# A linear-attention and feed-forward kernel on one core: its beginning in another order, and three operations on other engines

## The chip, the core and the metric

One core of a Trainium2 chip runs the whole program. The metric is the time of one execution on the device in microseconds (us), as a median over several executions; a profile of one execution shows what each engine did. The engines here are TensorE (PE, with its weight loads as PEld), VectorE (DVE), ScalarE (ACT), GpSimd (POOL) and SyncE (SP), which issues transfers; ACT's queue can issue transfers too (ACTq).

## The reference

```python
# attention: B=4, H=8, S=768, D=48
f = sigmoid(f_logit)
for t in range(S):
    state = f[:, :, t, :, None] * state + einsum('bhd,bhde', k[:, :, t], v[:, :, t])
    y[:, :, t] = einsum('bhd,bhde->bhe', q[:, :, t], state)
# feed-forward on x = y as (3072 tokens, 384 channels); d_ff = 1536
out = ((x @ w_a) * (x @ w_b)) @ w_out
```

q, k, v and f_logit come as 32-bit floats; w_a, w_b and w_out come as 64-bit floats (two 32-bit words each) and the kernel turns them into 32-bit floats itself.

## The kernel before

All work that runs is in `by_quotients` (a second function, `by_levels`, is a fallback for other data). The attention is cut into 16 **units** (4 batches, 2 halves of 384 tokens, 2 groups of 4 heads), numbered 0 to 15; two units make one **block** of 384 tokens for the feed-forward, so there are 8 blocks. Unit u's inputs lie in one of four sets of tiles (`f_in`, `k_in`, `q_in`, `v_in`).

A unit goes through these steps. `front(u)` has three parts: two sigmoids on ACT (L211, L212) and two products on POOL (L214, L215); then `fix` on ACT (L217), a running product of f on DVE (L220, a scan, two halves of 384 columns), a check value `held` (L221) and the product that scales q (L222), both on DVE; then a second scan (L226) and the product that scales k (L227) on DVE. `scores(u)` is 48 small matmuls (L251) into the PSUM tile `ps_x` and a product with a causal mask on DVE (L259). `turn(u)` transposes k on PE (L275) and copies it on ACT (L277 or L279). `gains(u)` makes the states (PE L294, DVE L308 to L317). `within(u)` (L327) and `across(u)` (L347) add up y in `ps_y`; ACT copies it out (L358) into the one buffer `y`, and five transfers (L372) put it into `xT`, which the feed-forward reads.

The weights come as 36 **pieces** of 128 by 384 values: 12 times one of w_b and one of w_a, then 12 of w_out. A piece is loaded into a `raw` tile by SP (`load_weights`, L153). `from_double` converts it in three stages, a generator that is advanced once per step of `conversion`: first |hi| and the sign on ACT (L165, L166) and a clamp on POOL (L167); then three operations on DVE (L171, L172, L173), an addition on POOL (L174) and |h| on ACT (L175); then the product with the sign on DVE (L178). A step of `conversion` starts one new piece, takes the second stage of the one before and the third of the one before that, and issues one further load, four pieces ahead. `convert(n)` runs steps until n pieces are done.

`ffn(blk)` has 12 steps for the two products (L387: w_b, then w_a), each ended by a copy `b_sb` on ACT (L395) and a product `ab` on DVE (L397), and then the product with w_out (L407), copied out (L417) and stored (L419, SP). In block 0 the conversion runs beside the feed-forward, two pieces per step at first and then one, and the w_out product goes by pieces too. The attention steps of the later units are put between the steps by a list of numbers (`queue`).

Every engine works through its own list in the order in which the code emits it, and so does SP with its transfers: one that has to wait holds all behind it. The code around the change is the beginning, which is written out by hand (L453 to L503):

```python
for _ in range(4): load_weights()
...
convert(0); next(fronts[0]); next(fronts[0]); scores(0); turn(0, True)
convert(1); next(fronts[1]); next(fronts[1]); within(0); gains(0)
for u in range(NQ, NSET): load_unit(u)
next(fronts[2]); scores(1); turn(1, True)
```

Of the kernel before, what the change touches and what calls it, by code (L numbers as in the profile page):

```python
# [10 lines left out]
FP32 = mybir.dt.float32  # L11
# [62 lines left out]
def by_quotients(ctx, tc, q, k, f_logit, v, moe_w_a, moe_w_b, moe_w_out, out, ident, weights, bad):  # L74
# [131 lines left out]
    def front(u):  # L206
# [35 lines left out]

    def scores(u):
        t = sets[u % NSET]
        qf, kf = halves(t["q"]), halves(t["k"])
        ps = ps_x
        for n, c, o in each():
            for h in range(2):
                for p in range(2):
                    r = slice(R * h, R * h + D)  # L250
                    nc.tensor.matmul(  # L251
                        ps[SUB * p:SUB * p + SUB, h, o:o + SUB],
                        lhsT=kf[r, tokens(n, c, p)],
                        rhs=qf[r, tokens(n, c, p)],
                        start=True,
                        stop=True,
                    )
        at = sb2.tile([128, 2, BLK], FP32, tag="at", name="at")
        nc.vector.tensor_tensor(  # L259
            at.rearrange("s h (o t) -> s h o t", t=SUB),  # L260
            ps[:, :, 0:BLK].rearrange("s h (o t) -> s h o t", t=SUB),
            causal.unsqueeze(1).unsqueeze(1).broadcast_to((128, 2, 2 * NC, SUB)),
            ALU.mult,
        )
        live[u]["at"] = at

    def turn(u, spare=False):

        kf = halves(sets[u % NSET]["k"])
        kT = sb1.tile([128, 2, NC, 128], FP32, tag="kT", name="kT")  # L270
        for n in range(2):
            ps = ps_f.tile([128, 512], FP32, tag="f", name="f") if spare else ps_x[:, n]
            for c in range(NC):
                o = n * BLK + c * C
                nc.tensor.transpose(ps[:, c * C:c * C + C], kf[:, o:o + C], ident)  # L275
            if spare:
                nc.scalar.copy(kT[:, n].rearrange("s c x -> s (c x)"), ps[:, 0:BLK])  # L277
# [58 lines left out]
    def across(u):  # L336
# [116 lines left out]
    with tc.manual_schedule():  # L453
        nc.scalar.preload_act_table_set("sigmoid_and_others")
        for x, value in ((less, -K_EXP), (two, 2.0), (zeros, 0.0)):
            nc.gpsimd.memset(x, value)
        for i in range(NSET):
            for n, eng, x in (("f", nc.vector, 30.0), ("k", nc.gpsimd, 0.0), ("q", nc.vector, 0.0)):
                eng.memset(sets[i][n], x)
            if i < NQ:  # L460
                load_unit(i, "f")
            if i == 0:
                make_identity(nc, ident)
        for u in range(NQ):
            load_unit(u, "kqv")
# [19 lines left out]
        next(fronts[0])
# [400 lines left out]
```

## Time and profile before

| | us |
|---|---|
| median of three runs (lowest, highest) | 754.71 (754.36, 755.13) |
| the profiled execution, its own time | 754.88 |
| its span, first to last instruction | 752.80 |
| PE busy | 643.6 (85%) |
| DVE busy | 277.3 (37%) |
| ACT busy | 182.6 (24%) |
| POOL busy | 114.0 (15%) |

The profiled execution took 2.08 us more than its span. A busy share is an average over stages that differ: in forty slices of the span PE is at 0 to 6 tenths in the first seven and at 9 tenths from the thirteenth on. The first matmul of the feed-forward (L387) starts at 83.44 us, and that of its second block at 213.26 us.

### The profile page before, as it was taken

Reading aid. Unit: us, or ns where it says so; the run is one execution under the profiler, and the core shown is the slowest. Engines: PE = TensorE matmul, PEld = TensorE weight load, DVE = VectorE, ACT = ScalarE, POOL = GpSimd, SP = SyncE. Lnnn points to the kernel's source line nnn. Section 1 sums busy time; section 2 is a strip of 40 time slices with the busy share of each in tenths; the row PEclk is TensorE's granted clock in tenths of the full one; section 3 lists DMA queues with packets and bytes.
Section 4 is the critical chain, followed back from the end, with each engine's and each line's share of the span. In section 5 each row is a group of like instructions: output and inputs, shape, how many; then the busy total and the mean of one; then the engine's idle time right before and its main releaser. Section 6 shows DMA issues by size and latency. Waiting matters only on the chain.

```text
span 752.8 us, 11345 instructions
## 1 busy us (share of the span) xinstructions
PE 643.6 (85%) x4770; PEld 392.3 (52%) x4770; DVE 277.3 (37%) x484; ACT 182.6 (24%) x343; POOL 114.0 (15%) x121
## 2 busy tenths in 40 slices
PE   0322665576989999999999999999999999999996
PEld 0312333343556666666666666665665666555553
DVE  7716867775933331334024313322342211101100
ACT  2232344443422211222022202221221111011100
POOL 5221454445520100110011001100101000000000
PEclk9655699879999999999999999999999999999999
DMA  8166333532421022012301040103000100010000
GB/s 209 44 157 166 83 89 104 149 100 84 125 79 43 7 77 66 10 39 60 84 0 49 27 115 1 49 6 105 1 18 1 37 11 17 1 38 11 1 11 24
DMA packets 34300, 43.29 MB, mean 58 GB/s; under 512 B 4032, under 2 KB 32704, under 8 KB 34240
## 3 DMA queue, kind: packets, MB, share of 16 engines
q1 hardware_dynamic: 29888, 37.76, 18.6%
q10 hardware_dynamic: 4352, 4.72, 2.4%
q8 instruction: 39, 0.64, 0.3%
q14 instruction: 21, 0.17, 0.1%
HBM read 33.03 MB, written 4.72 MB: 50 GB/s over the span
## 4 chain that ended last, share of the span: by engine, by line
PE 72%; POOL 9%; DVE 7%; ACT 4%; issue 4%; DMA 1%; ACTq 1%; SPq 1%; DVEq 0%; POOLq 0%
PE f L387 44%; PE f L407 22%; POOL h L174 6%; PE ps_x L251 2%; POOL h L167 2%; PE ps_y L327 2%; ACT h L165 1%; PE ps_y L347 1%; DVE r L173 1%; PE ps_x L294 1%; PE ps_x L275 1%; DVE f_in L220 1%; DVE r L172 1%; POOL fix L215 1%; ACTq L372 1%
## 5 line engine op out<-in xcount | busy, mean ns | idle before, releaser
L387 PE MATMUL f<-xT,w_b 128*128 128x384 f32 x576 | 214.4, 510 | 23.2 <-ACT b_sb L395 23.2
L387 PE MATMUL f<-xT,w_a 128*128 128x384 f32 x576 | 202.0, 487 | 0.0
L407 PE MATMUL f<-w_out,ab 128*128 128x384 f32 x576 | 190.3, 488 | 5.3 <-DVE w_out L178 3.5
L397 DVE TENSOR_TENSOR ab<-f,b_sb 128x384 f32<-128x384 f32 x96 | 53.5, 558 | 334.2 <-PE f L387 296.2
L387 PEld LDWEIGHTS f<-xT,w_b 128*128 128x128 f32 x576 | 110.7, 198 | 97.9 <-ACT b_sb L395 26.9
L407 PEld LDWEIGHTS f<-w_out,ab 128*128 128x128 f32 x576 | 108.4, 190 | 82.0 <-DVE w_out L178 6.3
L387 PEld LDWEIGHTS f<-xT,w_a 128*128 128x128 f32 x576 | 110.0, 191 | 77.3 <-issue 2.0
L395 ACT COPY b_sb<-f 128x384 f32<-128x384 f32 x96 | 45.8, 477 | 232.4 <-PE f L387 214.2
L214 POOL TENSOR_SCALAR inv<-inv 128x768 f32<-128x768 f32 x16 | 14.6, 915 | 357.0 <-ACT inv L212 356.9
L251 PE MATMUL ps_x<-q_in,k_in 48*64 48x64 f32 x768 | 17.3, 243 | 48.3 <-DVE k_in L227 25.9
L417 ACT COPY o_sb<-f 128x384 f32<-128x384 f32 x24 | 11.5, 479 | 162.8 <-PE f L407 161.4
L174 POOL TENSOR_TENSOR h<-h,r 128x384 f32<-128x384 f32 x36 | 44.4, 1234 | 23.7 <-DVE r L173 23.7
L251 PEld LDWEIGHTS ps_x<-q_in,k_in 48*64 48x64 f32 x768 | 15.6, 156 | 48.8 <-issue 40.1
L175 ACT ACTIVATE h<-h 128x384 f32<-128x384 f32 x36 | 18.8, 523 | 82.0 <-POOL h L174 79.3
L220 DVE TENSOR_TENSOR_SCAN f_in<-f,zeros 128x384 f32<-128x384 f32 x32 | 32.8, 1066 | 3.0 <-ACT inv L212 3.0
L167 POOL TENSOR_SCALAR h<-h 128x384 f32<-128x384 f32 x36 | 20.9, 582 | 70.1 <-ACT h L165 69.8
L215 POOL TENSOR_TENSOR fix<-f,inv 128x768 f32<-128x768 f32 x16 | 30.3, 1893 | 1.3
L171 DVE TENSOR_SCALAR h<-h 128x384 uint32<-128x384 uint32 x36 | 25.7, 714 | 12.2 <-POOL h L167 12.2
L226 DVE TENSOR_TENSOR_SCAN inv<-inv,fix 128x384 f32<-128x384 f32 x32 | 29.0, 948 | 0.0
L358 ACT COPY y<-ps_y 64x384 f32<-64x384 f32 (+1 forms) x48 | 22.8, 475 | 23.7 <-PE ps_y L347 23.2
L310 DVE TENSOR_TENSOR st<-st,ps_x 128x96 f32<-128x96 f32 x80 | 20.3, 253 | 21.7 <-PE ps_x L294 19.2
L327 PE MATMUL ps_y<-at,v_in 64*48 64x64 f32 x768 | 15.5, 231 | 12.7 <-ACT y L358 12.7
(49 smaller groups left out, 323.6 us busy)
## 6 DMA issues: line engine op xcount, KB each, us to landing
f_in<-in_f_logit_dram SPq DMA_DIRECT2D x32, 144.0 KB, 3.9
k_in<-in_k_dram SPq DMA_DIRECT2D x32, 144.0 KB, 3.8
q_in<-in_q_dram SPq DMA_DIRECT2D x32, 144.0 KB, 3.5
v_in<-in_v_dram SPq DMA_DIRECT2D x16, 288.0 KB, 4.0
raw<-in_moe_w_b_dram SPq DMA_DIRECT2D x12, 384.0 KB, 3.4
raw<-in_moe_w_a_dram SPq DMA_DIRECT2D x12, 384.0 KB, 3.5
raw<-in_moe_w_out_dram SPq DMA_DIRECT2D x12, 384.0 KB, 3.0
out_dram<-o_sb SPq DMA_DIRECT2D x24, 192.0 KB, 1.9
```

What stands on the lines that cost most here:

```text
L167: nc.gpsimd.tensor_scalar(h, h, HI_MAX, HI_MIN, ALU.min, ALU.max)
L171: nc.vector.tensor_scalar(hu, hu, 3, 0x40000000, ALU.logical_shift_left, ALU.bitwise_xor)
L174: nc.gpsimd.tensor_tensor(h, h, r, ALU.add)
L215: nc.gpsimd.tensor_tensor(fix, f, inv, ALU.mult)
L220: nc.vector.tensor_tensor_scan(x[:, c], f[:, c], zeros, math.exp(MIDDLE), ALU.mult, ALU.add)
L226: nc.vector.tensor_tensor_scan(inv[:, c], inv[:, c], fix[:, c], math.exp(-MIDDLE), ALU.mult, ALU.mult)
L251: nc.tensor.matmul(ps[SUB * p:SUB * p + SUB, h, o:o + SUB], lhsT=kf[r, tokens(n, c, p)], rhs=qf[r, tokens(n, c, p)], start=True, stop=True,)
L327: nc.tensor.matmul(ps_y[e:e + D, p, o:o + SUB], lhsT=t["v"][r, n, c, h * D:h * D + D], rhs=at[r, h, o:o + SUB], start=o == 0, stop=True, s ...
L387: nc.tensor.matmul(ps[nm], lhsT=w[:, kt, ft * 128:ft * 128 + 128], rhs=x[:, kt], start=kt == 0, stop=kt == NKT - 1,)
L395: nc.scalar.copy(b_sb, ps["b"])
L397: nc.vector.tensor_tensor(ab[ft], ps["a"], b_sb, ALU.mult)
L407: nc.tensor.matmul(o[tg], lhsT=ab[ft][:, tg * 128:tg * 128 + 128], rhs=w_out[:, ft], start=ft == 0, stop=ft == NFT - 1,)
```

## The change

Several edits in one diff. The fills and loads of units 0 and 1 come first, then two weight loads, then the loads of units 2 and 3 with one weight load behind each (they stood behind `convert(1)`, after seven weight loads). `raw` has five buffers and not four. The three parts of the fronts of units 0 and 1 are emitted in turns, ahead of the first pieces. `from_double` waits one step more between its first and its second stage; its addition goes to DVE and its product with the sign to POOL. The product that scales q goes from DVE to POOL in all units. `scores(1)` and `turn(1)` write to idle banks (`ps_f`) and not to `ps_x`, and `kT` has two buffers. The transfers from `y` to `xT` are issued by SP and no longer by ACT, in all units. `held` is made by a comparison of two tensors, and the scan's zeros are one broadcast column. `front(2)`'s first part stands behind `gains(1)`.

```diff
-    raw_pool = ctx.enter_context(tc.tile_pool(name="raw", bufs=4))
+    raw_pool = ctx.enter_context(tc.tile_pool(name="raw", bufs=5))
...
         nc.gpsimd.tensor_scalar(h, h, HI_MAX, HI_MIN, ALU.min, ALU.max)
         yield
+        yield
         r = sb2.tile([128, PIECE], FP32, tag="r", name="r")
...
-        nc.gpsimd.tensor_tensor(h, h, r, ALU.add)
+        nc.vector.tensor_tensor(h, h, r, ALU.add)
         nc.scalar.activation(h, h, AF.Abs)
         yield
...
-        nc.vector.tensor_tensor(dst, h, sign, ALU.mult)
+        nc.gpsimd.tensor_tensor(dst, h, sign, ALU.mult)
...
-        for n in range(len(todo) + 2):
+        for n in range(len(todo) + 3):
...
-            yield n - 1
+            yield n - 2
...
-        nc.vector.tensor_scalar(held[:, u], t["f"][:, :, BLK - 1], math.exp(MIDDLE - DECAY_MAX), None, ALU.is_ge)
-        nc.vector.tensor_tensor(halves(t["q"]), halves(t["q"]), x, ALU.mult)
+        nc.vector.tensor_tensor(held[:, u], t["f"][:, :, BLK - 1], least, ALU.is_ge)
+        nc.gpsimd.tensor_tensor(halves(t["q"]), halves(t["q"]), x, ALU.mult)
...
-    def scores(u):
+    def pair(spare=False):
+
+        return [ps_f.tile([128, 512], FP32, tag="f", name="f") if spare else ps_x[:, i] for i in range(2)]
+
+    def scores(u, spare=False):
...
-        kT = sb1.tile([128, 2, NC, 128], FP32, tag="kT", name="kT")
+        kT = sb2.tile([128, 2, NC, 128], FP32, tag="kT", name="kT")
+        ps = pair(spare)
...
-                    nc.scalar.dma_start(out=xT[blk][p:p + w, kt], in_=y[row:row + w, n])
+                    nc.sync.dma_start(out=xT[blk][p:p + w, kt], in_=y[row:row + w, n])
...
-        for _ in range(4):
-            load_weights()
+        load_weights()
+        load_weights()
+        for u in range(NQ, NSET):
+            for n, eng, x in (("f", nc.gpsimd, 30.0), ("k", nc.gpsimd, 0.0), ("q", nc.vector, 0.0)):
+                eng.memset(sets[u][n], x)
+            load_unit(u)
+            load_weights()
...
         next(fronts[0])
         next(fronts[1])
-        convert(0)
         next(fronts[0])
+        next(fronts[1])
         next(fronts[0])
+        next(fronts[1])
+        convert(1)
         scores(0)
         turn(0, True)
-        convert(1)
-        next(fronts[1])
-        next(fronts[1])
+        convert(2)
         within(0)
         gains(0)
-        for u in range(NQ, NSET):
-            load_unit(u)
-        next(fronts[2])
-        scores(1)
+        scores(1, True)
         turn(1, True)
-        convert(2)
+        convert(3)
         across(0)
         within(1)
         gains(1)
-        convert(3)
+        next(fronts[2])
+        convert(4)
+        across(1)
         next(fronts[2])
         next(fronts[2])
         slots = {s: slot(s) for s in range(NQ, NU + 1)}
         next(slots[NQ])
-        across(1)
         convert(6)
```

Three places show how the instructions move. The first is SP's list behind the loads of units 0 and 1. Names ending in 97, 96, 95 and 98 are unit 2's set, those in 101, 100, 99 and 102 unit 3's, those in 89, 88, 87 and 90 the first set again, for unit 4. Before:

```order
L131 DMA v_in_94<-in_v_dram 128x2x288
L153 DMA raw<-in_moe_w_b_dram 128x3x128
L153 DMA raw<-in_moe_w_a_dram 128x3x128
L153 DMA raw<-in_moe_w_b_dram 128x3x128
L153 DMA raw<-in_moe_w_a_dram 128x3x128
L153 DMA raw<-in_moe_w_b_dram 128x3x128
L153 DMA raw<-in_moe_w_a_dram 128x3x128
L153 DMA raw<-in_moe_w_b_dram 128x3x128
L129 DMA f_in_97<-in_f_logit_dram 48x2x384 x2
```

Now, the same list from the tenth weight load on, with the five transfers of unit 0's y, the loads of unit 4, one more weight load and unit 1's y:

```order
L154 DMA raw<-in_moe_w_a_dram 128x3x128
L381 DMA xT<-y 48x384 x2
L381 DMA xT<-y 32x384
L381 DMA xT<-y 16x384
L381 DMA xT<-y 48x384
L130 DMA f_in_89<-in_f_logit_dram 48x2x384 x2
L130 DMA k_in_88<-in_k_dram 48x2x384 x2
L130 DMA q_in_87<-in_q_dram 48x2x384 x2
L132 DMA v_in_90<-in_v_dram 128x2x288
L154 DMA raw<-in_moe_w_b_dram 128x3x128
L381 DMA xT<-y 48x384
```

Unit 2's loads stood behind seven weight loads and now stand behind two; the transfers of y, which were in ACT's list, stand in SP's behind weight loads that need a free `raw` buffer.

The second place is DVE's list at the beginning of unit 0 (`f_in_89`, `k_in_88`) and unit 1 (`f_in_93`, `k_in_92`). Before:

```order
L220 SCALAR_TENSOR_TENSOR f_in_89<-f,zeros 128x384 x2
L221 TENSOR_SCALAR held<-f_in_89 128x2
L222 TENSOR_TENSOR q_in_87<-q_in_87,f_in_89 128x768
L226 SCALAR_TENSOR_TENSOR inv<-inv,fix 128x384 x2
L227 TENSOR_TENSOR k_in_88<-k_in_88,inv 128x768
L259 TENSOR_TENSOR at<-ps_x,causal 128x768
L171 TENSOR_SCALAR h<-h 128x384
L172 TENSOR_SCALAR r<-h 128x384
L173 SCALAR_TENSOR_TENSOR r<-raw,r 128x384
```

Now:

```order
L222 SCALAR_TENSOR_TENSOR f_in_89<-f,zero 128x384 x2
L223 TENSOR_TENSOR held<-f_in_89,least 128x2
L222 SCALAR_TENSOR_TENSOR f_in_93<-f,zero 128x384 x2
L223 TENSOR_TENSOR held<-f_in_93,least 128x2
L228 SCALAR_TENSOR_TENSOR inv<-inv,fix 128x384 x2
L229 TENSOR_TENSOR k_in_88<-k_in_88,inv 128x768
L228 SCALAR_TENSOR_TENSOR inv<-inv,fix 128x384 x2
L229 TENSOR_TENSOR k_in_92<-k_in_92,inv 128x768
L173 TENSOR_SCALAR h<-h 128x384
L174 TENSOR_SCALAR r<-h 128x384
L175 SCALAR_TENSOR_TENSOR r<-raw,r 128x384
L176 TENSOR_TENSOR h<-h,r 128x384
```

Unit 1's part has come ahead of the first piece and of unit 0's mask product, the products with q are gone from this list, and a piece ends with the addition.

The third place is ACT's list around the copies of y of units 0 and 1 (`f_in_97` is unit 2's). Before:

```order
L175 ACTIVATE h<-h 128x384
L358 COPY y<-ps_y 128x6x64
L358 COPY y<-ps_y 64x6x64 x2
L372 DMA xT<-y 48x384 x2
L372 DMA xT<-y 32x384
L372 DMA xT<-y 16x384
L372 DMA xT<-y 48x384
L165 ACTIVATE h<-raw 128x384
```

Now:

```order
L177 ACTIVATE h<-h 128x384
L367 COPY y<-ps_y 128x6x64
L367 COPY y<-ps_y 64x6x64 x2
L213 ACTIVATE f<-f_in_97 128x768
L214 ACTIVATE inv<-f_in_97,less 128x768
L166 ACTIVATE h<-raw 128x384
L167 ACTIVATE sign<-raw 128x384
L177 ACTIVATE h<-h 128x384
L367 COPY y<-ps_y 128x6x64
L367 COPY y<-ps_y 64x6x64 x2
L219 ACTIVATE fix<-fix,two 128x768
```

ACT no longer issues the five transfers, and the second copy into the one `y` buffer stands ahead of unit 2's `fix`.

## Rows read from the trace of the kernel before

**Rows 1.** Busy time by stretch; columns: PE, PEld, DVE, ACT, POOL, granted clock, DMA.
```profile
0.00:83.40 83.40, 17.91 (x474) 16.00 (x474) 50.68 (x79) 26.39 (x46) 27.49 (x40) 0.65 0.58 145
83.40:213.30 129.90, 92.46 (x609) 52.82 (x606) 97.11 (x169) 55.48 (x114) 60.10 (x62) 0.89 0.35 99
213.30:752.80 539.50, 533.21 (x3693) 323.45 (x3691) 129.49 (x238) 100.70 (x183) 26.38 (x20) 1.00 0.12 34
```

**Rows 2.** Timeline of the beginning: start, us, engine, line, operation, idle before.
```profile
9.49 2.59 DVE L220 TENSOR_TENSOR_SCAN f_in<-f,zeros 128x384 f32<-128x384 f32 x2
...
38.84 1.09 SPq L129 DMA_DIRECT2D f_in<-in_f_logit_dram  x2
...
43.73 0.84 ACT L211 ACTIVATE f<-f_in 128x768 f32<-128x768 f32 x1 [14.22 <-DMA f_in<-in_f_logit_dram]
...
79.49 0.52 ACT L175 ACTIVATE h<-h 128x384 f32<-128x384 f32 x1 [1.45 <-POOL h L174]
...
83.44 4.03 PE L387 MATMUL f<-xT,w_b 128*128 128x384 f32 x6
```

**Rows 3.** Groups by line, 300 to 752 us: busy, mean ns of one, idle before.
```profile
L215 POOL TENSOR_TENSOR fix<-f,inv 128x768 f32<-128x768 f32 x8 | 14.4, 1806 | 0.7
L214 POOL TENSOR_SCALAR inv<-inv 128x768 f32<-128x768 f32 x8 | 6.7, 831 | 288.2 <-ACT inv L212 288.2
...
L220 DVE TENSOR_TENSOR_SCAN f_in<-f,zeros 128x384 f32<-128x384 f32 x16 | 14.4, 940 | 0.0
...
L222 DVE TENSOR_TENSOR q_in<-q_in,f_in 128x768 f32<-128x768 f32 x8 | 7.7, 958 | 0.0
```

**Rows 4.** Timeline of the conversion: one piece behind another, then one alone.
```profile
74.85 0.51 POOL L167 TENSOR_SCALAR h<-h 128x384 f32<-128x384 f32 x1 [1.08 <-ACT h L165]
74.89 0.87 DVE L178 TENSOR_TENSOR w_b<-h,sign 128x384 f32<-128x384 f32 x1
...
75.32 1.29 POOL L174 TENSOR_TENSOR h<-h,r 128x384 f32<-128x384 f32 x1
75.69 1.14 DVE L171 TENSOR_SCALAR h<-h 128x384 uint32<-128x384 uint32 x1
...
76.86 0.36 DVE L172 TENSOR_SCALAR r<-h 128x384 uint32<-128x384 uint32 x1
...
77.26 0.56 DVE L173 SCALAR_TENSOR_TENSOR r<-raw,r 128x384 f32<-128x384 uint32 x1
...
77.69 0.51 POOL L167 TENSOR_SCALAR h<-h 128x384 f32<-128x384 f32 x1 [1.08 <-ACT h L165]
...
206.56 0.36 DVE L171 TENSOR_SCALAR h<-h 128x384 uint32<-128x384 uint32 x1
...
207.83 0.55 DVE L178 TENSOR_TENSOR w_out<-h,sign 128x384 f32<-128x384 f32 x1
```

**Rows 5.** What DVE waited for, 9 to 213 us: total, times, longest.
```profile
DVE ab L397 <- ACT b_sb L395: 21.7, 12, 1.8
```

**Rows 6.** Timeline of block 0: two plain steps, then the transfers of y.
```profile
131.22 0.46 ACT L395 COPY b_sb<-f 128x384 f32<-128x384 f32 x1
...
138.34 0.46 ACT L395 COPY b_sb<-f 128x384 f32<-128x384 f32 x1
138.70 1.47 ACT L358 COPY y<-ps_y 128x384 f32<-128x384 f32 x3
...
139.70 3.10 ACTq L372 DMA_DIRECT2D xT<-y  x5
...
143.50 0.51 POOL L167 TENSOR_SCALAR h<-h 128x384 f32<-128x384 f32 x1 [5.62 <-ACT h L165]
...
210.05 0.52 ACT L175 ACTIVATE h<-h 128x384 f32<-128x384 f32 x1 [2.68 <-DMA xT<-y]
```

**Rows 7.** Timeline before block 2: the last y of it and its first matmul.
```profile
275.81 3.66 ACTq L372 DMA_DIRECT2D xT<-y  x5
...
290.78 1.45 PE L387 MATMUL f<-xT,w_b 128*128 128x384 f32 x4
```

More of the change, by code (lines that the diff above doesn't have):

```diff
@@ L107, in by_quotients @@
     causal = fixed([128, SUB], "causal")
-    zeros = fixed([128, BLK], "zeros")
+    zero = fixed([128, 1], "zero")
+    least = fixed([128, 2], "least")
     ones = fixed([128, 1], "ones")
@@ L219, in front @@
             c = slice(n * BLK, n * BLK + BLK)
-            nc.vector.tensor_tensor_scan(x[:, c], f[:, c], zeros, math.exp(MIDDLE), ALU.mult, ALU.add)
-        nc.vector.tensor_scalar(held[:, u], t["f"][:, :, BLK - 1], math.exp(MIDDLE - DECAY_MAX), None, ALU.is_ge)
-        nc.vector.tensor_tensor(halves(t["q"]), halves(t["q"]), x, ALU.mult)
+            nc.vector.tensor_tensor_scan(x[:, c], f[:, c], zero.broadcast_to((128, BLK)), math.exp(MIDDLE), ALU.mult, ALU.add)
+        nc.vector.tensor_tensor(held[:, u], t["f"][:, :, BLK - 1], least, ALU.is_ge)
+        nc.gpsimd.tensor_tensor(halves(t["q"]), halves(t["q"]), x, ALU.mult)
         yield
@@ L241, in each @@
                 yield n, c, (n * NC + c) * SUB
-    def scores(u):
+    def pair(spare=False):
+        return [ps_f.tile([128, 512], FP32, tag="f", name="f") if spare else ps_x[:, i] for i in range(2)]
+    def scores(u, spare=False):
         t = sets[u % NSET]
         qf, kf = halves(t["q"]), halves(t["k"])
-        ps = ps_x
+        ps = pair(spare)
         for n, c, o in each():
@@ L251, in scores @@
                     nc.tensor.matmul(
-                        ps[SUB * p:SUB * p + SUB, h, o:o + SUB],
+                        ps[h][SUB * p:SUB * p + SUB, o:o + SUB],
                         lhsT=kf[r, tokens(n, c, p)],
@@ L258, in scores @@
         at = sb2.tile([128, 2, BLK], FP32, tag="at", name="at")
[L259 to L264, printed above, removed]
+        both = [(at[:, h], ps[h][:, 0:BLK]) for h in range(2)] if spare else [(at, ps_x[:, :, 0:BLK])]
+        for to, x in both:
+            lead = x.shape[1:-1]
+            letters = "h"[:len(lead)]
+            to, x = (y.rearrange(f"s {letters} (o t) -> s {letters} o t", t=SUB) for y in (to, x))
+            tri = causal.unsqueeze(1)
+            for _ in lead:
+                tri = tri.unsqueeze(1)
+            nc.vector.tensor_tensor(to, x, tri.broadcast_to((128, *lead, 2 * NC, SUB)), ALU.mult)
         live[u]["at"] = at
@@ L269, in turn @@
         kf = halves(sets[u % NSET]["k"])
-        kT = sb1.tile([128, 2, NC, 128], FP32, tag="kT", name="kT")
+        kT = sb2.tile([128, 2, NC, 128], FP32, tag="kT", name="kT")
+        ps = pair(spare)
         for n in range(2):
-            ps = ps_f.tile([128, 512], FP32, tag="f", name="f") if spare else ps_x[:, n]
             for c in range(NC):
                 o = n * BLK + c * C
-                nc.tensor.transpose(ps[:, c * C:c * C + C], kf[:, o:o + C], ident)
+                nc.tensor.transpose(ps[n][:, c * C:c * C + C], kf[:, o:o + C], ident)
             if spare:
-                nc.scalar.copy(kT[:, n].rearrange("s c x -> s (c x)"), ps[:, 0:BLK])
+                nc.scalar.copy(kT[:, n].rearrange("s c x -> s (c x)"), ps[n][:, 0:BLK])
         if not spare:
@@ L454, in by_quotients @@
         nc.scalar.preload_act_table_set("sigmoid_and_others")
-        for x, value in ((less, -K_EXP), (two, 2.0), (zeros, 0.0)):
+        for x, value in ((less, -K_EXP), (two, 2.0), (zero, 0.0), (least, math.exp(MIDDLE - DECAY_MAX)), (ones, 1.0)):
             nc.gpsimd.memset(x, value)
[L457 to L465, printed above, removed]
+        for names in ("f", "kqv"):
+            for u in range(NQ):
+                for n, eng, x in (("f", nc.vector, 30.0), ("k", nc.gpsimd, 0.0), ("q", nc.vector, 0.0)):
+                    if n in names:
+                        eng.memset(sets[u][n], x)
+                load_unit(u, names)
         for ps in (ps_x, ps_y):
             nc.vector.memset(ps, 0.0)
+        load_weights()
+        load_weights()
+        for u in range(NQ, NSET):
+            for n, eng, x in (("f", nc.gpsimd, 30.0), ("k", nc.gpsimd, 0.0), ("q", nc.vector, 0.0)):
+                eng.memset(sets[u][n], x)
+            load_unit(u)
+            load_weights()
+        done = [0]
+        fronts = [front(u) for u in range(NQ + 1)]
+        next(fronts[0])
+        next(fronts[1])
+        make_identity(nc, ident)
         nc.gpsimd.memset(causal, 1.0)
@@ L473, in by_quotients @@
             )
-        nc.gpsimd.memset(ones, 1.0)
-        done = [0]
-        for _ in range(4):
-            load_weights()
-        fronts = [front(u) for u in range(NQ + 1)]
         next(fronts[0])
         next(fronts[1])
-        convert(0)
         next(fronts[0])
-        next(fronts[0])
+        next(fronts[1])
+        convert(1)
         scores(0)
         turn(0, True)
-        convert(1)
-        next(fronts[1])
-        next(fronts[1])
+        convert(2)
         within(0)
         gains(0)
-        for u in range(NQ, NSET):
-            load_unit(u)
-        next(fronts[2])
-        scores(1)
+        scores(1, True)
         turn(1, True)
-        convert(2)
+        convert(3)
         across(0)
```

## The prediction, made before the changed kernel ran

> **What bounds the kernel now.** I read busy time by stretch first, cut at the first matmul of the feed-forward and at that of its second block [rows 1]. The stretches differ. In the last, 539.5 us long, PE is busy 533.2 us at the full clock: matmul bounds it, and no edit touches that list's length. In the middle one, block 0, 129.9 us, PE is busy 92.5 us, part of it at the lower clock (granted 0.89 on average); the blocks behind take about 77 us each (539.5 / 7). In the first, 83.4 us, PE is busy 17.9 us. There DVE is busy 50.7 and POOL 27.5 us: together 78.2 of 83.4, nearly a sum, as if the two took turns. So some 65 to 130 us of the beginning are not matmul, and that is where the change works.
>
> Why the first stretch is long is in the timeline [rows 2]. Unit 2's first load is issued at 38.84 us, behind weight loads that wait for a `raw` buffer; its sigmoid starts at 43.73, after ACT sat 14.22 us idle for it. Everything of unit 2, which stands ahead of the first L387 in PE's list, is late by that.
>
> Block 0 goes at the pace of the conversion. One piece behind another takes 2.84 us (clamp at 74.85, next clamp at 77.69) [rows 4], though DVE's four operations alone take 0.36 + 0.36 + 0.56 + 0.55 = 1.83 us and POOL's two 0.51 + about 0.9. There is a loop: ACT's |h| waits for POOL's addition, the next clamp waits for ACT (POOL idle 1.08 us each time), the next addition stands behind that clamp. But DVE is not free either: L171 takes 1.14 us when the addition runs and 0.36 when POOL is idle, L178 0.87 beside the clamp and 0.55 alone. Its end follows POOL's end: the addition ends at 76.61, L171 at 76.83. The two engines exclude each other, operation by operation. In each feed-forward step DVE further waits 1.81 us for `b_sb` (21.7 us in 12 waits) [rows 5], since that copy stands behind ACT's |h|, behind POOL's addition.
>
> The Trainium skill, "SBUF — State Buffer", section "SBUF: two separate sides", says the port pair that DVE and GpSimd share is an exclusive lock, held for the whole instruction, against DVE operations with two SBUF inputs or in a two-port mode. The trace agrees (1.14 against 0.36 us). That rule speaks against hoping for a faster pace from swapping an addition and a product of one shape between the engines; what it does in full is a rival below.
>
> **The beginning, to the first L387.** I work by a budget of DVE and POOL that take turns, up to the same place in the program (second stage of piece 6).
> - The first scan starts at 9.49 us now [rows 2]; two of the ten fills ahead of it on DVE leave that engine, about 0.8 us each, so it starts near 8.
> - Three fronts. DVE: four scans of 0.94 and k's product of 0.96, 4.7 us; POOL: 0.83 + 1.81 [rows 3], and q's product, which the trace does not show on POOL; L215 is a product of the same shape there, so 1.81 against 0.96 on DVE. Bounds: 0.96 and 2.4. One front is 4.7 + 4.45 = 9.15, three are 27.5.
> - Seven pieces. The addition and the product change places, both are a tensor product or sum of 128 by 384, so I take the same 0.55 on DVE and 0.9 on POOL. Taking turns: 1.83 + 0.51 + 0.9 less about 0.5 that lies outside the overlap = 2.75, seven 19.
> - Mask products and states of units 0 and 1 and the mask product of unit 2, about 7 us by DVE's share of what is left of its 50.7 us.
> - Sum 8 + 27.5 + 19 + 7 = 61.5. From the last |h| to the first L387 before is 83.44 - 79.49 = 3.95 [rows 2]; the same four things stand there after. So 65.5 if DVE and POOL never both idle.
>
> They will, once: the new wait. Unit 0's five transfers of y stand in SP's list behind the tenth weight load, which needs the buffer of piece 4, so they cannot go before DVE's third operation of piece 4; ACT's second copy into the one `y` buffer waits for them to land, and unit 2's `fix`, its second scan, k, scores and mask product are queued behind. The transfers take 3.1 us to issue [rows 6] and some 2 to land; I put the idle time at 3.5 us. The waits for unit 2's load (14.2 us) go, since it now stands ahead of all weight loads but two. Sum 69, so -14.4 us. Lower bound 62: POOL's work hidden under DVE's waits for PE. Upper bound 78: each of the hand-overs ACT, PE, SP, DVE adds its wait.
>
> **Block 0.** Same place to same place, 129.9 us.
> - A plain step takes 138.34 - 131.22 = 7.12 us [rows 6]. Now |h| waits for DVE's own sum, not POOL's, so after the last sum come |h| (0.52) and `b_sb` (0.46) and the wait is 1.0 us and not 1.81. POOL's product of the piece before can run in that wait. The pace itself I leave at 2.84: the loop over ACT and POOL is gone, with a step more between the clamp and its reader, but turns of 2.75 remain. I take -0.7 per step; 12 steps, -8.4. Bounds: nothing, and -1.9 (2 x 1.83 + 0.56 + 1.0 = 5.2 us per step), if POOL and DVE did not exclude each other.
> - The five transfers on ACT: 3.10 us twice in block 0, with POOL idle 5.62 us behind the first and |h| 2.68 us behind the second [rows 6]. On SP they hold no conversion; weight loads behind them were issued four pieces (11 us) ahead. -2.5 each, -5. Bounds -2.5 and -6.
> - q's product on POOL: 0.85 us more of the turns, for three fronts 2.5, half of it in a wait: +1.3. Bounds 0 and +2.5.
> - Sum 129.9 - 8.4 - 5 + 1.3 = 117.8. It stays above PE's 92.5 us of work, so PE doesn't take over.
>
> The Trainium skill, "GPSIMD Engine Reference", section "Engine selection", puts an elementwise product on VectorE, with GpSimd about twice as slow for two inputs; the rows give 1.81 against 0.96 for q, which agrees. By that rule alone the move of q is a loss of 0.85 us per unit.
>
> **The rest.** From the second block on PE bounds: 539.5 unchanged. The cover for q's slower product is the slot list, which takes a unit through its front in 7.5 steps of a block of about 77 us; the cover for y on SP is the 290.78 - 279.47 = 11.3 us between the end of issue and the block that needs it [rows 7]. Without that cover each boundary would pay the excess. `held`, the broadcast zeros and the spare banks cost nothing beyond this.
>
> **Sum.** 69 + 117.8 + 539.5 = 726.3 of span, and 754.88 - 752.80 = 2.08 around it: 728.4, against 754.88 profiled, -26.5 us (3.5%). The profiled run is 0.17 us above the median of the runs, so 728.
>
> **Rivals.**
> - *The lock eats the pace.* POOL's clamp and product come in DVE's way as often as the addition did, and with unit 1's front beside unit 0's and q on POOL, in full. For: DVE's 1.14 against 0.36. Against: POOL's idle 1.08 us per piece and DVE's 1.81 per step show room. Then the start is 75 (halfway to the bound of 78), block 0 keeps its steps and loses only the y transfers less q, 127: 75 + 127 + 539.5 + 2.1 = 744.
> - *Little exclusion.* POOL's product finds gaps, a step is 5.2 us, the w_out pieces come at 1.83 to 2: block 0 goes down to PE's own 92.5 and some waits, 97; the start is 62: 701. Against: every long L171.
> - *Not different.* The conversion is started early but its last piece is no earlier, because another list (SP's loads at the beginning, 6.3 MB at 145 GB/s mean [rows 1] is 43 us) holds pieces: 754.
> - *Slower.* y on SP is held at each block boundary by what stands ahead of it there, stores of the output that wait for PE. Against: y stands ahead of the block's last two stores. If it stood behind them it would land some 6 us too late, 7 times 6 on top of 728: 770. It decides against the change from 11.3 us (the cover) and 26.5 / 7 = 3.8, so 15 us of hold per boundary.
>
> **How the numbers follow.** Chances: my forecast 0.6, its own range 716 to 738 (the bounds of the beginning and the smaller bounds of block 0, not all at one end); the lock 0.2; little exclusion 0.1; not different 0.05; slower 0.05. I predict 728. A range of 711 to 745 holds the forecast, the lock and the upper edge of little exclusion, and leaves out some 0.2. This kernel's runs differ by 0.1%, so 0.2% (1.5 us) is about what can be told from no change: faster 0.9, same 0.05, slower 0.05.
>
> **What would show it.** The first L387 near 69 us, and ACT's idle time ahead of unit 2's sigmoid gone. DVE's waits for `b_sb` near 1.0 us in 12 steps, plain steps near 6.4 us, the piece's period still 2.7 to 2.9 with L173's successor long beside POOL's product. No idle POOL of 5 us behind y. The second block near 187 us, and 539.5 us from there, PE without new waits. I am wrong if the first L387 is later than 78 or earlier than 62, if pieces come at 2 us or over 3, or if a block boundary shows PE waiting for y.

## The result, and the profile after

The changed kernel takes 728.02 us (median of 4 runs, 727.65 to 728.63) against 754.75 us beside it: a ratio of 0.9647, 95% interval 0.963 to 0.9663, 26.7 us less. The profiled execution took 727.83 us, its span 726.10.

First the busy time by stretch of the changed kernel, cut at the same two matmuls (now L396; [rows 1] is cut within 0.04 us of them); columns as in [rows 1].

```profile
0.00:68.97 68.97, 18.08 (x474) 15.91 (x474) 51.66 (x76) 27.58 (x48) 38.81 (x46) 0.77 0.63 163
68.97:186.79 117.82, 90.00 (x607) 51.51 (x606) 102.36 (x165) 55.39 (x112) 66.09 (x65) 0.90 0.38 110
186.79:726.10 539.31, 533.20 (x3693) 323.45 (x3691) 120.24 (x227) 100.49 (x184) 44.41 (x30) 1.00 0.14 35
```

Against [rows 1] the beginning went from 83.40 to 68.97 us (-14.4), block 0 from 129.90 to 117.82 (-12.1), the rest from 539.50 to 539.31. All of the gain lies where matmul doesn't bound. Note DVE and POOL in the beginning: 51.66 + 38.81 = 90.5 us in a stretch of 69.0. Part of the time the two work side by side, and an operation that is held counts as busy meanwhile (1.14 against 0.36 us for one and the same operation in [rows 4]). So the sum of the two is no lower bound of the stretch.

The timeline of the beginning of the changed kernel:

```profile
7.92 3.30 DVE L222 TENSOR_TENSOR_SCAN f_in<-f,zero 128x384 f32<-128x384 f32 x2
...
22.97 1.07 DVE L229 TENSOR_TENSOR k_in<-k_in,inv 128x768 f32<-128x768 f32 x1
...
38.31 1.44 ACT L367 COPY y<-ps_y 128x384 f32<-128x384 f32 x3
39.78 0.84 ACT L213 ACTIVATE f<-f_in 128x768 f32<-128x768 f32 x1
...
41.54 0.83 POOL L216 TENSOR_SCALAR inv<-inv 128x768 f32<-128x768 f32 x1 [4.69 <-ACT inv L214]
...
42.37 0.26 DVE L317 COPY st<-ps_x 128x96 f32<-128x96 f32 x1 [4.52 <-PE ps_x L303]
...
46.19 0.56 DVE L175 SCALAR_TENSOR_TENSOR r<-raw,r 128x384 f32<-128x384 uint32 x1
...
46.82 0.37 SPq L154 DMA_DIRECT2D raw<-in_moe_w_a_dram  x1
...
47.28 3.12 SPq L381 DMA_DIRECT2D xT<-y  x5
...
52.23 1.46 ACT L367 COPY y<-ps_y 128x384 f32<-128x384 f32 x3 [4.33 <-DMA xT<-y]
53.71 0.94 ACT L219 ACTIVATE fix<-fix,two 128x768 f32<-128x768 f32 x1
...
54.68 2.07 DVE L228 TENSOR_TENSOR_SCAN inv<-inv,fix 128x384 f32<-128x384 f32 x2 [5.43 <-ACT fix L219]
...
65.03 0.52 ACT L177 ACTIVATE h<-h 128x384 f32<-128x384 f32 x1 [0.64 <-DVE h L176]
...
68.97 3.40 PE L396 MATMUL f<-xT,w_b 128*128 128x384 f32 x6
```

Unit 2's sigmoid (39.78) no longer waits: the 14.22 us of [rows 2] are gone. A new chain has come. Unit 0's y is copied by 39.75, but its transfers go at 47.28, behind a weight load that waits for L175 at 46.19. ACT's second copy waits for them, `fix` stands behind the copy, and DVE idles 5.43 us for it.

Block 0 of the changed kernel, two plain steps and the copy of y:

```profile
111.86 0.46 ACT L404 COPY b_sb<-f 128x384 f32<-128x384 f32 x1
...
118.11 0.46 ACT L404 COPY b_sb<-f 128x384 f32<-128x384 f32 x1
118.47 1.46 ACT L367 COPY y<-ps_y 128x384 f32<-128x384 f32 x3
...
120.59 0.51 POOL L168 TENSOR_SCALAR h<-h 128x384 f32<-128x384 f32 x1 [2.09 <-ACT h L166]
```

What DVE waited for, 7 to 190 us:

```profile
DVE ab L406 <- ACT b_sb L404: 11.5, 12, 1.0
```

A plain step is 118.11 - 111.86 = 6.25 us and was 7.12. Of the 0.87 less, 0.85 is the wait for `b_sb` (11.5 / 12 = 0.96 here, 1.81 before; [rows 5]): without it a step is 5.3 us in both kernels. POOL's idle time behind y is 2.09 and was 5.62 [rows 6].

Block 0 has two parts that behave differently: up to the last copy of `b_sb`, and the w_out pieces behind it. The last copy before, then now:

```profile
184.60 0.46 ACT L395 COPY b_sb<-f 128x384 f32<-128x384 f32 x1
```

```profile
158.24 0.46 ACT L404 COPY b_sb<-f 128x384 f32<-128x384 f32 x1
```

The first part went from 101.16 us (184.60 - 83.44) to 89.27 (158.24 - 68.97), the second from 28.66 (213.26 - 184.60) to 28.55 (186.79 - 158.24): all of block 0's gain is in the twelve steps.

The chain that ended last (start, us, what) shows the pace where the w_out pieces follow one another:

```profile
172.97 1.08 DVE h L173
...
175.81 1.09 DVE h L173
```

The two are 2.84 us apart, as in [rows 4]; L173 is still the long one.

### The profile page after: what moved, and what is told of

Same layout as the page of the kernel before. It is cut to its first block, busy times and chain, and to the rows that moved or that the text cites. A ratio compares the mean times of both kernels' runs of the same rounds, so it can differ in the third digit from the quotient of the medians.

```text
span 726.1 us, 11432 instructions
## 1 busy us (share of the span) xinstructions
PE 641.3 (88%) x4770; PEld 390.9 (54%) x4770; DVE 274.3 (38%) x467; ACT 183.5 (25%) x343; POOL 149.3 (21%) x140
## 4 chain that ended last, share of the span: by engine, by line
PE 74%; DVE 16%; ACT 3%; POOL 2%; DMA 2%; issue 2%; SPq 0%; ACTq 0%; POOLq 0%
PE f L396 45%; PE f L416 23%; DVE h L176 3%; DVE r L175 3%; DVE r L174 2%; DVE h L173 2%; DMA k_in<-in_k_dram 2%; PE ps_y L336 2%; DVE inv L228 1%; PE ps_x L257 1%; PE ps_y L356 1%; DVE f_in L222 1%; PE ps_x L303 1%; PE ps_x L284 1%; DVE st L319 1%
## 5 line engine op out<-in xcount | busy, mean ns | idle before, releaser
L396 PE MATMUL f<-xT,w_b 128*128 128x384 f32 x576 | 212.4, 507 | 14.9 <-ACT b_sb L404 14.9
L396 PE MATMUL f<-xT,w_a 128*128 128x384 f32 x576 | 201.7, 486 | 0.0
L396 PEld LDWEIGHTS f<-xT,w_b 128*128 128x128 f32 x576 | 109.7, 196 | 88.3 <-POOL w_a L180 11.2
L396 PEld LDWEIGHTS f<-xT,w_a 128*128 128x128 f32 x576 | 109.9, 191 | 77.3 <-issue 1.6
L216 POOL TENSOR_SCALAR inv<-inv 128x768 f32<-128x768 f32 x16 | 14.6, 914 | 236.5 <-ACT inv L214 236.4
L426 ACT COPY o_sb<-f 128x384 f32<-128x384 f32 x24 | 11.5, 478 | 167.8 <-PE f L416 162.2
L224 POOL TENSOR_TENSOR q_in<-q_in,f_in 128x768 f32<-128x768 f32 x16 | 30.6, 1915 | 107.6 <-DVE f_in L222 102.1
L257 PE MATMUL ps_x<-q_in,k_in 48*64 48x64 f32 x720 | 15.5, 238 | 41.4 <-POOL q_in L224 19.8
L257 PEld LDWEIGHTS ps_x<-q_in,k_in 48*64 48x64 f32 x720 | 13.9, 152 | 41.9 <-POOL q_in L224 19.8
L228 DVE TENSOR_TENSOR_SCAN inv<-inv,fix 128x384 f32<-128x384 f32 x32 | 33.9, 1100 | 5.4 <-ACT fix L219 5.4
L168 POOL TENSOR_SCALAR h<-h 128x384 f32<-128x384 f32 x36 | 22.9, 638 | 53.6 <-ACT h L166 51.3
L222 DVE TENSOR_TENSOR_SCAN f_in<-f,zero 128x384 f32<-128x384 f32 x32 | 32.4, 1054 | 2.1 <-ACT inv L214 2.1
L217 POOL TENSOR_TENSOR fix<-f,inv 128x768 f32<-128x768 f32 x16 | 31.2, 1950 | 1.3
L367 ACT COPY y<-ps_y 64x384 f32<-64x384 f32 (+1 forms) x48 | 22.8, 474 | 21.0 <-PE ps_y L356 16.1
L176 DVE TENSOR_TENSOR h<-h,r 128x384 f32<-128x384 f32 x36 | 26.8, 746 | 1.2
L175 DVE SCALAR_TENSOR_TENSOR r<-raw,r 128x384 f32<-128x384 uint32 x36 | 25.3, 703 | 1.2
```

What stands on the lines that cost most here:

```text
L176: nc.vector.tensor_tensor(h, h, r, ALU.add)
L217: nc.gpsimd.tensor_tensor(fix, f, inv, ALU.mult)
L222: nc.vector.tensor_tensor_scan(x[:, c], f[:, c], zero.broadcast_to((128, BLK)), math.exp(MIDDLE), ALU.mult, ALU.add)
L224: nc.gpsimd.tensor_tensor(halves(t["q"]), halves(t["q"]), x, ALU.mult)
L228: nc.vector.tensor_tensor_scan(inv[:, c], inv[:, c], fix[:, c], math.exp(-MIDDLE), ALU.mult, ALU.mult)
L257: nc.tensor.matmul(ps[h][SUB * p:SUB * p + SUB, o:o + SUB], lhsT=kf[r, tokens(n, c, p)], rhs=qf[r, tokens(n, c, p)], start=True, stop=True,)
```

## The experiments

"My theory" in the expectations is the prediction's working. The ratios are to the kernel before, which took 755.0 to 755.3 us beside these runs. Except where the text says so, a kernel is the changed one with one edit.

### y back on ACT

```diff
-                    nc.sync.dma_start(out=xT[blk][p:p + w, kt], ...
+                    nc.scalar.dma_start(out=xT[blk][p:p + w, kt], ...
```

> The changed kernel with one line back: the five transfers of y are issued by ACT again. My theory: block 0 gets back 2 x 2.5 us behind the two y transfers in it, and the beginning gives up about 1 us (the transfers of unit 0's y no longer wait behind the tenth weight load, but ACT spends 3.1 us on issuing them, twice): 728 + 4 = 732. Rival 1, the move to SP is worth nothing: 728. Rival 2, the wait in SP's list costs more at the beginning than ACT's time in block 0: 724.

730.67 us, 0.9676 (0.9662 to 0.9689): between my 732 and the rival's 728. The beginning is 69.09, block 0 121.00 (+3.2). Its timeline, first where the changed kernel has the rows from 118.47 on, then at the second y:

```profile
119.60 3.16 ACTq L381 DMA_DIRECT2D xT<-y  x5
...
123.45 0.62 POOL L168 TENSOR_SCALAR h<-h 128x384 f32<-128x384 f32 x1 [4.82 <-ACT h L166]
...
185.36 1.21 POOL L180 TENSOR_TENSOR w_out<-h,sign 128x384 f32<-128x384 f32 x1 [3.56 <-ACT h L177]
...
186.62 3.63 PE L416 MATMUL f<-w_out,ab 128*128 128x384 f32 x6 [2.56 <-POOL w_out L180]
```

The same matmuls in the changed kernel:

```profile
184.75 2.20 PE L416 MATMUL f<-w_out,ab 128*128 128x384 f32 x6 [1.72 <-POOL w_out L180]
```

The hold of [rows 6] is back, but costs 0.9 us the first time (up to the last `b_sb` copy, 90.19 for 89.27) and 2.3 the second (behind it, 30.81 for 28.55). The first time, DVE has two clamped pieces in hand: it starts their first operations at 120.52 and 122.37, without a wait for POOL. The second time, no further piece is left. ACT's |h| and POOL's product come late, PE is idle 2.56 us for 1.72, and 1.4 of the 2.3 us come after that: the last six matmuls take 3.63 us for 2.20. Busy time and granted clock there (columns as in [rows 1]):

```profile
186.60:190.09 3.49, 3.47 (x7) 2.00 (x8) 0.78 (x1) 0.96 (x2) 0.00 (x0) 0.58 0.14 45
```

It is 0.58 on average, so most of these 3.5 us went at 1.2 GHz; the changed kernel has 1.00 (2.4 GHz) from 184.70 to 186.79.

The beginning is as long either way: what ACT saves of the wait behind SP's weight load it seems to lose by issuing; I did not take the two apart.

### Addition back on POOL, product back on DVE

```diff
-        nc.vector.tensor_tensor(h, h, r, ALU.add)
+        nc.gpsimd.tensor_tensor(h, h, r, ALU.add)
...
-        nc.gpsimd.tensor_tensor(dst, h, sign, ALU.mult)
+        nc.vector.tensor_tensor(dst, h, sign, ALU.mult)
```

> The changed kernel with the addition on POOL and the product with the sign on DVE, as before; the additional step stays. My theory: the turns of a piece are the same sum, so pieces that follow one another directly stay at 2.84 us, but b_sb waits for ACT's |h|, which waits for POOL again: DVE's wait for b_sb goes from 0.96 back to 1.8 us, 12 x 0.7 = 8 us in block 0, 2 at the beginning: 738. Rival, the additional step did it all: 728 to 729.

740.56 us, 0.9808 (0.9791 to 0.9824), for 738 expected: the extra step alone does not bring it. The beginning is 71.92 (+3.0), block 0 128.82 (+11.0). DVE's waits for `b_sb`, all in block 0:

```profile
DVE ab L406 <- ACT b_sb L404: 22.8, 12, 2.4
```

That is 11.3 us more than after, as much as block 0 lost. Behind the last `b_sb` copy (172.42) nothing is lost: 28.32 us.

### Without the extra step

```diff
         yield
-        yield
         r = sb2.tile([128, PIECE], FP32, tag="r", name="r")
...
-        for n in range(len(todo) + 3):
+        for n in range(len(todo) + 2):
...
-            yield n - 2
+            yield n - 1
```

> The changed kernel without the additional step between the clamp and its reader. My theory: the addition on DVE alone has opened the loop over ACT and POOL, so the pace stays; and unit 0's y now stands behind the ninth weight load, which needs piece 3 (third operation on DVE at 36.0 us) and not piece 4 (46.2 us), so ACT's wait of 4.3 us for its landing goes: 728 - 4 = 724, plain steps still 6.2 to 6.4 us. Rival, the additional step is what opened the loop: plain steps go back to 7 us and the time to 735 or more.

726.34 us, 0.9617 (0.9604 to 0.963), for 724 expected. The beginning is 64.75 (-4.2): y now stands behind a weight load that needs an earlier piece. But block 0 is 121.07 (+3.25), where I had expected no change. The timeline shows why (its line numbers are one lower: L172 is L173 above, L215 and L216 are L216 and L217):

```profile
85.43 0.88 POOL L215 TENSOR_SCALAR inv<-inv 128x768 f32<-128x768 f32 x1 [1.72 <-ACT inv L213]
...
86.39 2.00 POOL L216 TENSOR_TENSOR fix<-f,inv 128x768 f32<-128x768 f32 x1
...
88.47 0.51 POOL L168 TENSOR_SCALAR h<-h 128x384 f32<-128x384 f32 x1
...
89.01 1.14 DVE L172 TENSOR_SCALAR h<-h 128x384 uint32<-128x384 uint32 x1 [2.30 <-POOL h L168]
```

The clamp stands behind a unit's front on POOL, and DVE waits for it. In block 0 DVE waits for the clamp 4.6 us here (twice) and waited 6.2 in the kernel before (three times); in the changed kernel it doesn't. That is what the extra step is for.

### Late loads of units 2 and 3

```diff
                 eng.memset(sets[u][n], x)
-            load_unit(u)
             load_weights()
...
         gains(0)
+        for u in range(NQ, NSET):
+            load_unit(u)
         scores(1, True)
```

> The changed kernel with the loads of units 2 and 3 back behind the conversion's steps (behind nine weight loads, ahead of unit 1's scores). What the prediction put on this edit: ACT's 14 us of waiting for unit 2's load come back, 742. Against it, in the changed order pieces come earlier, so the ninth weight load gets its buffer at 37 us and unit 2's f would land near 41 or 42, where its sigmoid starts at 39.8 now; and weight loads 3 and 4 would land at 16 to 18 us and not at 22.8 and 28.3: 728 to 732.

729.77 us, 0.9669 (0.9653 to 0.9685): only 1.7 us, the beginning 71.13. My account of the 14.2 us fails here. The loads are issued as late as in the kernel before, yet the wait is small; the timeline:

```profile
37.56 0.96 SPq L130 DMA_DIRECT2D f_in<-in_f_logit_dram  x2
...
42.22 0.84 ACT L213 ACTIVATE f<-f_in 128x768 f32<-128x768 f32 x1 [2.64 <-DMA f_in<-in_f_logit_dram]
```

The diff also puts front 2's first part behind `gains(1)`; ACT gets there at 39.6 us, so most of the former wait goes by on items that now stand ahead of it. With either edit most of the wait is gone, so undoing one costs little. The new place of front 2 alone, in the kernel before, was not run.

### The early loads alone, in the kernel before

```diff
         done = [0]
-        for _ in range(4):
+        load_weights()
+        load_weights()
+        for u in range(NQ, NSET):
+            load_unit(u)
             load_weights()
...
         gains(0)
-        for u in range(NQ, NSET):
-            load_unit(u)
         next(fronts[2])
```

> The kernel before with one edit alone: the loads of units 2 and 3 stand behind two weight loads, with one weight load behind each, as in the changed kernel. If the 14.2 us that ACT waited for unit 2's load were all that made the beginning long, as the prediction had it: first matmul of the feed-forward at 70 to 72 us, 742. Against it: taking this edit out of the changed kernel cost 1.7 us only, so other things are as late: 748 to 752, with the first matmul at 76 to 80.

745.35 us, 0.9869 (0.9853 to 0.9884), between the two expectations. The beginning is 74.26 (-9.1), block 0 130.19. Its timeline:

```profile
29.47 0.83 ACT L211 ACTIVATE f<-f_in 128x768 f32<-128x768 f32 x1
...
37.52 1.06 ACT L277 COPY kT<-f 128x384 f32<-128x384 f32 x2 [6.40 <-PE f L275]
...
41.10 1.44 ACT L358 COPY y<-ps_y 128x384 f32<-128x384 f32 x3
```

The same two copies in the kernel before:

```profile
45.31 0.84 ACT L277 COPY kT<-f 128x384 f32<-128x384 f32 x2
...
50.21 1.45 ACT L358 COPY y<-ps_y 128x384 f32<-128x384 f32 x3
```

Unit 2's sigmoid is 14.3 us earlier than at 43.73 [rows 2], the first L387 only 9.2. The 5 us are lost right behind the sigmoid: the next item of ACT's list is the copy of unit 1's transposed k, and for that ACT now waits 6.40 us. Unit 1's transposes end no earlier than before (38.07 us, 37.59 before). From the copy of y on, both kernels run alike, 9.1 to 9.2 us apart. The 14.22 us of idle time hid a second wait, which takes over when the first goes.

### Unit 1's front where it was

```diff
         next(fronts[0])
-        next(fronts[1])
         next(fronts[0])
-        next(fronts[1])
...
         convert(2)
+        next(fronts[1])
+        next(fronts[1])
```

> The changed kernel with unit 1's front where it was, behind unit 0's scores and the first pieces. By the budget of DVE and POOL that take turns the order of the same work hardly matters: 728 to 730. Rival, what made the beginning short is unit 1's front beside unit 0's, since DVE works in the stretch in which the loads of weights still land: first matmul 8 us later, 736.

731.42 us, 0.9685 (0.9672 to 0.9699); the beginning 72.64 (+3.7), block 0 117.8. Neither figure fits: the order of the same work matters more than the budget of turns has it (728 to 730), and less than the rival said (736). DVE now waits twice for a `fix` (10.0 us in all, 5.4 in the changed kernel).

### The swap alone, in the kernel before

```diff
-        nc.gpsimd.tensor_tensor(h, h, r, ALU.add)
+        nc.vector.tensor_tensor(h, h, r, ALU.add)
...
-        nc.vector.tensor_tensor(dst, h, sign, ALU.mult)
+        nc.gpsimd.tensor_tensor(dst, h, sign, ALU.mult)
```

> The kernel before with one edit alone: the addition on DVE and the product with the sign on POOL, with no additional step. My theory: DVE's wait for b_sb goes from 1.8 to 1.0 us and POOL's product runs in it, 0.7 to 0.9 us in each of 12 steps, less what the missing additional step costs (3 us in the changed kernel); 2 us at the beginning: 754.9 - 8 = 747. If the exclusion made the swap worthless by itself: 754 to 755.

745.16 us, 0.986 (0.9845 to 0.9875). The beginning is 79.52 (-3.9), block 0 124.94 (-5.0), for 747 expected. DVE's waits in block 0:

```profile
DVE ab L397 <- ACT b_sb L395: 11.5, 12, 1.0
DVE h L171 <- POOL h L167: 6.1, 3, 2.3
```

The `b_sb` wait falls by 10.2 us, as after, but block 0 by half of that. Up to the last `b_sb` copy (173.66) it is 7.0 us shorter (94.14 for 101.16) and not 10.2: DVE's operations take longer, 100.9 us in all of block 0 for 97.0. Behind that copy it is 2.1 us longer (30.80 for 28.66), in the way of y on ACT above: the last product, now on POOL, waits 3.56 us for an |h| that y's transfers hold, PE idles 2.57 us, and its last six matmuls take 3.74 us at a granted clock of 0.56. DVE's wait for the clamp is what it was (6.1 for 6.2 us); the extra step removes that.

### q's product back on DVE

```diff
-        nc.gpsimd.tensor_tensor(halves(t["q"]), halves(t["q"]), x, ALU.mult)
+        nc.vector.tensor_tensor(halves(t["q"]), halves(t["q"]), x, ALU.mult)
```

> The changed kernel with q's product on DVE again. My theory, DVE and POOL take turns: 0.85 us less of turns for each unit, five of them ahead of the second block, and the 4.98 us that two scans take beside two products on POOL shrink: 728 - 3 = 725. Rival, DVE's own list is the bound and q's product had been taken off it: 5 x 0.96 us more, 732.

727.07 us, 0.9629 (0.9612 to 0.9646). The interval overlaps that of the changed kernel, so by the time nothing can be told; the profile has the beginning at 69.27 (+0.3) and block 0 at 117.0 (-0.8). Neither 725 nor 732 lies in the interval.

### A second product on POOL, and two fills on POOL

The first kernel does POOL's product of a piece twice, with the same values; the second fills the product's place with zeros twice ahead of it.

```diff
+        nc.gpsimd.tensor_tensor(dst, h, sign, ALU.mult)
         nc.gpsimd.tensor_tensor(dst, h, sign, ALU.mult)
```

```diff
+        for _ in range(2):
+            nc.gpsimd.memset(dst, 0.0)
         nc.gpsimd.tensor_tensor(dst, h, sign, ALU.mult)
```

> The changed kernel with POOL's product with the sign done twice for each piece (the second writes the same values): 36 times about 1.0 us more on POOL, which has 0.7 to 2.1 us idle per piece. If DVE and POOL take turns: pieces that follow one another directly go from 2.84 to 3.7 us, plain steps from 6.25 to 7.2 or more, 29 pieces in block 0 less what the wait for b_sb hides: +18 to +24 us, 746 to 752. If POOL's work only matters for those who wait for it: 728 to 731.

> The changed kernel with two fills of the piece's place on POOL ahead of its product: 36 times about 0.8 us more on POOL, which write but read nothing. If any POOL operation takes its turn against every DVE operation: +15 to +20 us, 743 to 748. If two-input operations on DVE are held only by POOL operations that read: the 0.36 us operations (L173, L174) alone can be held, +2 to +8 us, 730 to 736. If POOL's time doesn't matter: 728.

The product: 749.34 us, 0.9922 (0.9905 to 0.9938), block 0 137.98 (+20.2, 0.70 us for each of its 29 pieces), a plain step 7.42 (6.25 without it). POOL's extra work goes into DVE's pace, as turns demand. The fills: 735.53 us, 0.9739 (0.9723 to 0.9756), block 0 124.03 (+6.2). DVE's groups in block 0 of the changed kernel, then of the one with fills (count, busy, mean ns):

```profile
L176 DVE TENSOR_TENSOR h<-h,r 128x384 f32<-128x384 f32 x29 | 22.6, 778 | 1.0
...
L174 DVE TENSOR_SCALAR r<-h 128x384 uint32<-128x384 uint32 x29 | 15.0, 518 | 1.0
```

```profile
L176 DVE TENSOR_TENSOR h<-h,r 128x384 f32<-128x384 f32 x29 | 21.8, 750 | 1.0
L174 DVE TENSOR_SCALAR r<-h 128x384 uint32<-128x384 uint32 x29 | 19.5, 673 | 1.0
```

With fills the operations with one input are longer (L174 673 for 518 ns, L173 656 for 585), not those with two (L176 750 for 778, L175 689 for 715). These are means; single operations beside a fill are in the last section.

### Two buffers for y, and with q on DVE

`kT` goes to one buffer to make the room. The second kernel has q's edit as well.

```diff
-        kT = sb2.tile([128, 2, NC, 128], FP32, tag="kT", name="kT")
+        kT = sb1.tile([128, 2, NC, 128], FP32, tag="kT", name="kT")
...
-        y = sb1.tile([128, 2 * NC, 2, SUB], FP32, tag="y", name="y")
+        y = sb2.tile([128, 2 * NC, 2, SUB], FP32, tag="y", name="y")
```

> The changed kernel with two y buffers, and one kT buffer (the memory for it). My theory: ACT's copy of unit 1's y no longer waits 4.33 us for the landing of unit 0's, so unit 2's fix, second scan, scores and the first matmul of the feed-forward come 3 to 4 us earlier: 724 to 725. Rival, unit 2 is bound by DVE's list anyway, or unit 1's y, behind piece 5 in SP's list, becomes the last thing that the first matmul waits for: 727 to 728.

> The changed kernel with two y buffers (one of kT) and q's product on DVE, the two edits that were faster alone (by 4 and by 1 us). If they add up, as DVE's and POOL's turns and ACT's wait are apart from each other: 723. If q's product on DVE now stands in the chain that the wait covered: 724 to 726.

The first: 724.03 us (723.38 to 724.52), 0.9585 (0.9572 to 0.9598): the beginning is 65.62 (-3.35), block 0 117.75. That is the price of the new wait, forecast at 3.5, net of whatever the one `kT` buffer costs. Both edits: 722.49 us (721.31 to 722.75), 0.9565 (0.9552 to 0.9578), with block 0 at 117.0. That is faster than the changed kernel; against the second `y` alone the two intervals just overlap.

## Why the prediction was right

The forecast (728, from 69 + 117.8 + 539.5 + 2.1) came true in each sum: 68.97, 117.82, 539.31 and 1.73 us. The steps under the sums held less evenly.

- **Beginning, first scan, tail and new wait.** The scan starts at 7.92 (forecast 8); from the last |h| to the first matmul are 68.97 - 65.03 = 3.94 us (3.95); ACT waits 4.33 us for y, worth 3.35 when taken away (3.5).
- **Beginning, fronts and idle time.** The two early fronts end at 24.04 and began at 7.92: 16.1 us for 18.3 forecast. The budget let DVE and POOL both idle only once. They also do so near 38 to 41 us, DVE for PE's L303 and POOL for unit 2's sigmoid (idle 4.52 and 4.69). These two errors lie on opposite sides, so part of the agreement to 0.1 us is luck.
- **"The waits for unit 2's load (14.2 us) go."** They went, but the step named them alone as what the early loads bring, and they don't add up so: the early loads bring 9.2 us in the kernel before, since ACT then waits 6.40 us for PE, and taking them out of the changed kernel loses 2.2. The swap brings 3 to 4 us of the beginning, unit 1's early front 3.7. These overlap; the exact split isn't settled, and single undos can't settle it.
- **Block 0, steps.** Forecast -0.7 per step with a pace left alone; measured -0.87 in a plain one, of which 0.85 is the `b_sb` wait, and a pace of 2.84 as before. With the first y and q, about -9.6 was forecast for the twelve steps (-8.4, -2.5, +1.3); they gave -11.9. What the forecast didn't see is that DVE also waits for the clamp, 6.2 us in block 0, which the swap leaves and the extra step removes. Swap alone (-5.0) and the step when undone last (3.25) come to -8.3, near the -8.4, but that shows little: the swap when undone last is 11.0, so the shares depend on the order.
- **Block 0, y.** Taking y off ACT is worth 3.2 for 5 forecast: 0.9 for the first y, 2.3 for the second. And the 2.3 are no gain over the kernel before. Behind the last `b_sb` copy block 0 takes 28.66 us there (y on ACT, product on DVE), 30.8 with the product on POOL (with and without the other edits), and 28.55 when y goes to SP as well; with y on SP and the product on DVE it is 28.32 (that kernel has the extra step and q on POOL too). So -2.5 was forecast for this part and -0.1 came: the move of y there makes good what the swap would cost. The steps gave 2.3 us more than forecast and this part 2.4 less, and so the agreement of 117.82 with 117.8 is in good part luck.
- **Block 0, q.** +0.8 for +1.3; between the bounds, and no more than that can be said. An undisturbed q takes 1804 ns on POOL after 300 us (7 of them), for 1.81 forecast.
- **Not tried alone.** The fifth `raw` buffer, the spare banks of unit 1's scores (its transposes wrote to `ps_f` before, too), the order of the fills and the new place of front 2. What each of them brings is open.
- **The rest.** Unchanged, and y is issued by 253.15 us for a block that begins at 264.27: 11.1 us of cover for 11.3 forecast.
- **Two readings of the kernel before.** "65 to 130 us" that are not matmul should be 103: 65.5 in the beginning and 37.4 in block 0. And "nearly a sum, as if the two took turns" is no proof of turns: the same sum is 90.5 us in a beginning of 69.0 now. That the engines exclude each other rests on single operations ([rows 4] and the last section).
- **The rivals.** *The lock eats the pace* is refuted by the 6.25 us step, though its mechanism is real: with a second product on POOL the time is 749. *Little exclusion* is refuted by 2.84 us per piece. *Not different* had the loads as the limit; in the changed kernel the longest wait for a load is ACT's 5.09 us at 22.82. *Slower* is refuted by the cover.

## What to carry to other kernels

Where two engines hold each other up, moving an operation between them need not change the pace: here it stayed at 2.84 us per piece, and the move paid by what then stood behind what, 0.85 us less of a wait in each step. The same move can cost elsewhere: at the end of block 0 it was 2.1 us, until y's transfers left ACT's list. A wait in the trace can hide another one: 14.2 us were worth 9.2 alone, and 2.2 beside other edits that cover it. When a transfer moves to another queue, look at what it stands behind there and at the buffer that it frees: a second buffer was worth 3.35 us more. And a wait of PE can cost more than its own length: behind one of 2.56 us for 1.72, six matmuls took 3.63 us for 2.20, at the lower clock.

## What the runs showed of the hardware

POOL's fills did not hold DVE operations with two inputs in SBUF. In the kernel with fills (L181 is the two fills, L182 the product with the sign):

```profile
125.56 1.10 POOL L181 MEMSET w_b<- 128x384 f32 x2
125.86 0.56 DVE L175 SCALAR_TENSOR_TENSOR r<-raw,r 128x384 f32<-128x384 uint32 x1
126.45 0.56 DVE L176 TENSOR_TENSOR h<-h,r 128x384 f32<-128x384 f32 x1
...
179.24 1.19 POOL L181 MEMSET w_out<- 128x384 f32 x2
179.54 0.54 DVE L174 TENSOR_SCALAR r<-h 128x384 uint32<-128x384 uint32 x1
...
180.52 1.01 POOL L182 TENSOR_TENSOR w_out<-h,sign 128x384 f32<-128x384 f32 x1
180.71 1.23 DVE L176 TENSOR_TENSOR h<-h,r 128x384 f32<-128x384 f32 x1
```

L175 runs wholly beside the fills in its 0.56 us, and L176 begins beside them and takes 0.56; beside the product, which reads, L176 takes 1.23. The one-input L174 takes 0.54 beside the fills for 0.36 undisturbed. The Trainium skill, "SBUF — State Buffer", section "SBUF: two separate sides", says that a DVE operation with two SBUF inputs takes the shared lock only against a GpSimd operation that reads SBUF; the trace agrees.

Where one of two inputs is in PSUM, a read on POOL doesn't hold DVE either. The timeline of the kernel with a second product (its L181 is that product, its L407 the `ab` product, with `f` in PSUM):

```profile
171.54 1.00 POOL L181 TENSOR_TENSOR w_out<-h,sign 128x384 f32<-128x384 f32 x1
171.56 0.56 DVE L407 TENSOR_TENSOR ab<-f,b_sb 128x384 f32<-128x384 f32 x1 [0.96 <-ACT b_sb L405]
...
172.04 0.72 DVE L173 TENSOR_SCALAR h<-h 128x384 uint32<-128x384 uint32 x1
```

L407 takes its 0.56 us wholly beside POOL's product (all twelve L407 of block 0 take 0.56), and L173, begun 0.5 us before that product ends, takes 0.72 for 0.36.
